# Attention per head pair with weight sums inverted through DMA, and an MLP woven in by hand

## The chip, the cores and the metric

The kernel runs on one core of one Trainium2 chip. The metric is the device time of one execution in microseconds (us), from the first to the last instruction on that core. The engines of the core are named as the profile names them: PE (TensorE, matmuls; PEld is its weight loading), DVE (VectorE), ACT (ScalarE), POOL (GpSimd) and SP (SyncE, which here only issues transfers). Each engine takes its instructions in one fixed order; an instruction that waits holds up everything behind it on that engine.

## The reference

Softmax attention for 8 batches of 12 heads (448 tokens, 64 values a head), and a two-layer MLP with a leaky ReLU over the 3584 tokens that come out, 768 to 2048 to 768. All inputs and the output are fp32.

```python
def _attn_ref(q, k, v):                      # (8, 12, 448, 64) each
    scale = 1.0 / np.sqrt(q.shape[-1])
    scores = scale * np.matmul(q, k.transpose(0, 1, 3, 2))
    scores = scores - np.max(scores, axis=-1, keepdims=True)
    attn = np.exp(scores)
    attn = attn / (np.sum(attn, axis=-1, keepdims=True) + 1e-09)
    return np.matmul(attn, v).astype(np.float32)

def _moe_ref(x, w_in, w_out):                # x (3584, 768), w_in (768, 2048), w_out (2048, 768)
    h = x @ w_in
    g = np.maximum(0.01 * h, h)
    return (g @ w_out).astype(np.float32)
```

The inputs are small (q, k and v are normal draws times 0.1), and neither kernel subtracts the row maximum.

## The kernel before

Both weight matrices are loaded first, one transfer each, from POOL's queue, which casts fp32 to bf16 on the way. Then a loop over the 8 batches: `attn_batch(b)` traces the attention of batch b, and `mlp_batch(b - 1)` the MLP of the batch before. The order on each engine is made by the framework's scheduler from the dependencies; so matmuls of the MLP fill gaps of the attention, but no line of the kernel says where.

Attention goes by head pairs (`hp`, 6 a batch). For each head, q, k and v come by one casting transfer each (L77, L81, L85), 112 tokens on the partitions in four chunks (`so`); the tile of v also gets 64 columns of ones (L75). q and k of the two heads lie side by side, so a transpose by PE (L94, L97) of a 112 x 128 chunk puts head 0 on partitions 0 to 63 and head 1 on 64 to 127; DVE copies each chunk out (L95, L98). Then for each head: four score matmuls, keys down and queries across, over 64 rows of the array (L106); each is followed by Exp on ACT (L112); four matmuls of values with Exp's output (L117) gather in `pvpsum`, where rows 64 to 127 hold the sum of the weights 64 times over, from the ones. The sum is inverted on ACT as exp(-ln(sum)) (L126, L128), and DVE multiplies (L129) into `xT`, the transposed attention output.

The MLP of a batch (448 tokens) has 16 groups of six matmuls (L140) with Prelu on ACT (L146), and then eight groups of 16 matmuls (L151), each giving 112 tokens by 384 outputs, copied by DVE (L158) and stored from SP's queue (L159).

All PSUM pools have two buffers: `ps_tr` (transposes), `ps_sc` (scores), `ps_pv` (values) and `ps_mm` (MLP).

Of the kernel before, what the change touches and what calls it, by code (L numbers as in the profile page):

```python
# [1 line left out]

# [6 lines left out]

F32 = mybir.dt.float32  # L10
BF16 = mybir.dt.bfloat16
AX = mybir.ActivationFunctionType


@with_exitstack
def kernel(
    ctx: ExitStack,
    tc: tile.TileContext,
    q: bass.AP,
    k: bass.AP,  # L20
    v: bass.AP,
    moe_w_in: bass.AP,
    moe_w_out: bass.AP,
    out: bass.AP,
):
    nc = tc.nc

    B, H, S, D = q.shape
    DM, DF = moe_w_in.shape
    NTOK = B * S  # L30
    assert H * D == DM

    P = 128
    HP = H // 2
    SC = 112
    NSC = S // SC
    KD = DM // P
    MD = DF // P
    scale = 1.0 / float(D) ** 0.5

    const_pool = ctx.enter_context(tc.tile_pool(name="const", bufs=1))
    w_pool = ctx.enter_context(tc.tile_pool(name="weights", bufs=1))

    ident = const_pool.tile([P, P], BF16)
    make_identity(nc, ident)

    w_in_sb = w_pool.tile([P, KD, DF], BF16)
    nc.gpsimd.dma_start(
        out=w_in_sb, in_=moe_w_in.rearrange("(ko ki) n -> ki ko n", ki=P)
    )  # L50
    w_out_sb = w_pool.tile([P, MD, DM], BF16)
    nc.gpsimd.dma_start(
        out=w_out_sb, in_=moe_w_out.rearrange("(ko ki) n -> ki ko n", ki=P)
    )

    ld_pool = ctx.enter_context(tc.tile_pool(name="ld", bufs=2))
    qkT_pool = ctx.enter_context(tc.tile_pool(name="qkT", bufs=2))
    exp_pool = ctx.enter_context(tc.tile_pool(name="exp", bufs=2))
    pv_pool = ctx.enter_context(tc.tile_pool(name="pv", bufs=3))
    xT_pool = ctx.enter_context(tc.tile_pool(name="xT", bufs=2))  # L60
    h_pool = ctx.enter_context(tc.tile_pool(name="h", bufs=2))
    o_pool = ctx.enter_context(tc.tile_pool(name="o", bufs=4))

    ps_tr = ctx.enter_context(tc.tile_pool(name="ps_tr", bufs=2, space=bass.MemoryType.PSUM))
    ps_sc = ctx.enter_context(tc.tile_pool(name="ps_sc", bufs=2, space=bass.MemoryType.PSUM))
    ps_pv = ctx.enter_context(tc.tile_pool(name="ps_pv", bufs=2, space=bass.MemoryType.PSUM))
    ps_mm = ctx.enter_context(tc.tile_pool(name="ps_mm", bufs=2, space=bass.MemoryType.PSUM))

    def attn_batch(b, xT):
        for hp in range(HP):  # L70
            h0 = 2 * hp
            q_sb = ld_pool.tile([SC, NSC, 2, D], BF16, tag="q")
            k_sb = ld_pool.tile([SC, NSC, 2, D], BF16, tag="k")
            v_sb = ld_pool.tile([SC, NSC, 2, 2 * D], BF16, tag="v")
            nc.vector.memset(v_sb[:, :, :, D:], 1.0)  # L75
            for jh in range(2):
                nc.gpsimd.dma_start(  # L77
                    out=q_sb[:, :, jh, :],
                    in_=q[b, h0 + jh].rearrange("(so si) d -> si so d", si=SC),
                )  # L80
                nc.gpsimd.dma_start(  # L81
                    out=k_sb[:, :, jh, :],
                    in_=k[b, h0 + jh].rearrange("(so si) d -> si so d", si=SC),
                )
                nc.gpsimd.dma_start(  # L85
                    out=v_sb[:, :, jh, :D],
                    in_=v[b, h0 + jh].rearrange("(so si) d -> si so d", si=SC),
                )

            qT_sb = qkT_pool.tile([P, S], BF16, tag="qT")  # L90
            kT_sb = qkT_pool.tile([P, S], BF16, tag="kT")
            for so in range(NSC):
                qps = ps_tr.tile([P, SC], BF16, tag="tr")
                nc.tensor.transpose(qps, q_sb[:, so], ident[:SC, :SC])  # L94
                nc.vector.tensor_copy(qT_sb[:, ts(so, SC)], qps)  # L95
                kps = ps_tr.tile([P, SC], BF16, tag="tr")
                nc.tensor.transpose(kps, k_sb[:, so], ident[:SC, :SC])  # L97
                nc.vector.tensor_copy(kT_sb[:, ts(so, SC)], kps)  # L98

            for jh in range(2):  # L100
                h = h0 + jh
                pl = jh * D
                expT = exp_pool.tile([SC, NSC, S], BF16)
                for so in range(NSC):
                    spsum = ps_sc.tile([SC, S], F32, tag="sc")
                    nc.tensor.matmul(  # L106
                        spsum,
                        kT_sb[pl:pl + D, ts(so, SC)],
                        qT_sb[pl:pl + D, :],
                        start=True, stop=True,  # L110
                    )
                    nc.scalar.activation(  # L112
                        expT[:, so, :], spsum, AX.Exp, scale=scale
                    )
                pvpsum = ps_pv.tile([2 * D, S], F32, tag="pv")
                for so in range(NSC):
                    nc.tensor.matmul(  # L117
                        pvpsum,
                        v_sb[:, so, jh, :],
                        expT[:, so, :],  # L120
                        start=(so == 0), stop=(so == NSC - 1),
                    )
                kc = h // 2
                po = (h % 2) * D
                lns = pv_pool.tile([D, S], F32, tag="lns")
                nc.scalar.activation(lns, pvpsum[D:, :], AX.Ln)  # L126
                rec = pv_pool.tile([D, S], F32, tag="rec")
                nc.scalar.activation(rec, lns, AX.Exp, scale=-1.0)  # L128
                nc.vector.tensor_mul(  # L129
                    xT[po:po + D, kc, :], pvpsum[:D, :], rec  # L130
                )

    def mlp_batch(b, xT):
        NN = 2
        NW = DM // NN
        h_sb = h_pool.tile([P, MD, S], BF16)
        for m in range(MD):
            mpsum = ps_mm.tile([P, S], F32, tag="mm")
            for kk in range(KD):
                nc.tensor.matmul(  # L140
                    mpsum,
                    w_in_sb[:, kk, ts(m, P)],
                    xT[:, kk, :],
                    start=(kk == 0), stop=(kk == KD - 1),
                )
            nc.scalar.activation(h_sb[:, m, :], mpsum, AX.Prelu, alpha=0.01)  # L146
        for sq in range(NSC):
            for n in range(NN):
                opsum = ps_mm.tile([SC, NW], F32, tag="mm")
                for m in range(MD):  # L150
                    nc.tensor.matmul(  # L151
                        opsum,
                        h_sb[:, m, ts(sq, SC)],
                        w_out_sb[:, m, ts(n, NW)],
                        start=(m == 0), stop=(m == MD - 1),
                    )
                osb = o_pool.tile([SC, NW], F32, tag="osb")
                nc.vector.tensor_copy(osb, opsum)  # L158
                nc.sync.dma_start(  # L159
                    out=out[ds(b * S + sq * SC, SC), ts(n, NW)], in_=osb  # L160
                )

    xTs = [None] * B
    for b in range(B):
        xTs[b] = xT_pool.tile([P, KD, S], BF16, name="xT")
        attn_batch(b, xTs[b])
        if b > 0:
            mlp_batch(b - 1, xTs[b - 1])
    mlp_batch(B - 1, xTs[B - 1])


# [28 lines left out]
```

## Time and profile before

| what | number |
|---|---|
| three runs | 921.73, 922.72, 918.97 us; median 921.73 |
| profiled execution, its span | 923.2 us; no other time of its own is given |
| PE busy | 807.8 us (88%), 2944 matmuls |
| ACT busy | 592.9 us (64%), 193 of its 897 instructions are table loads |
| DVE, POOL busy | 181.9 us (20%), 203.3 us (22%) |
| mean granted TensorE clock | 0.752 |
| read from HBM, written | 45.61 MB, 11.01 MB |

The page of the profile is of one execution. Its shares of busy time are averages over stages with different limits. Further views used below: the chain of work that ended last, the groups of instructions by line, a table of busy time by stretch with the clock that PE was granted, and the instructions in order of time, where a bracket at the end of a row gives the idle time of the engine before it and who ended it.

### The profile page before, as it was taken

To read this page: it belongs to the slowest core of one execution; us is meant where nothing else is said; L and a number is where in the kernel's file an instruction comes from. 1 tells how busy PE (TensorE), PEld (TensorE's weight loads), DVE (VectorE), ACT (ScalarE), POOL (GpSimd) and SP (SyncE) were. 2 spreads that over 40 slices of the span, in tenths; PEclk is the share of its full clock that TensorE was granted. 3 is DMA by queue.
4 is the path that set the end of the run, shared out by engine and by line. 5 is a ranking of instruction groups with operands and counts; after the bars stand their busy time and mean duration, and the time that the engine had idled before them with its cause. 6 is when DMAs were issued, how large, how long until landed. Compare 5 with 4: busy or idle time off the path is not lost.

```text
span 923.2 us, 8367 instructions
## 1 busy us (share of the span) xinstructions
PE 807.8 (88%) x2944; PEld 336.8 (36%) x2944; DVE 181.9 (20%) x592; ACT 592.9 (64%) x897; POOL 203.3 (22%) x296
## 2 busy tenths in 40 slices
PE   0477789989899999999899998999989999999998
PEld 0122222236222552226322372224622255222656
DVE  0122212112212122211221122211222112120101
ACT  0188888871888538882688808886288844888130
POOL 3323232211332023210323103320132202310000
PEclk9999999979555895559755596557955588555999
DMA  9944343313443144322434115431343314410102
GB/s 179 141 25 29 25 31 20 26 12 65 29 30 21 27 59 31 20 16 43 47 26 30 11 53 42 26 20 18 63 30 26 20 28 58 30 11 0 43 18 60
DMA packets 144713, 34.36 MB, mean 37 GB/s; under 512 B 134688, under 2 KB 143904, under 8 KB 144672
## 3 DMA queue, kind: packets, MB, share of 16 engines
q0 software_dynamic: 136480, 22.83, 31.9%
q1 hardware_dynamic: 8192, 11.01, 4.0%
q8 instruction: 23, 0.38, 0.2%
q14 instruction: 18, 0.15, 0.1%
HBM read 45.61 MB, written 11.01 MB: 61 GB/s over the span
## 4 chain that ended last, share of the span: by engine, by line
PE 55%; ACT 33%; issue 6%; DMA 3%; POOL 1%; DVE 0%; POOLq 0%; ACTq 0%
PE opsum L151 18%; PE spsum L106 13%; PE mpsum L140 12%; ACT L112 12%; PE pvpsum L117 10%; ACT expT L112 9%; ACT lns L126 5%; ACT L126 4%; DMA q_sb<-in_q_dram 3%; PE qps L94 1%; ACT L128 1%; ACT h_sb L146 1%; PE kps L97 1%; ACT rec L128 0%; DVE v_sb L75 0%
## 5 line engine op out<-in xcount | busy, mean ns | idle before, releaser
L112 ACT ACTIVATE expT<-spsum 112x448 bf16<-112x448 f32 x384 | 195.1, 535 | 219.2 <-PE spsum L106 218.1
L140 PE MATMUL mpsum<-xT,w_in_sb 128*128 128x448 bf16 x768 | 287.3, 486 | 8.8 <-ACT h_sb L146 8.7
L106 PE MATMUL spsum<-qT_sb,kT_sb 64*112 64x448 bf16 x384 | 216.9, 569 | 66.0 <-ACT expT L112 65.8
L117 PE MATMUL pvpsum<-expT,v_sb 112*128 112x448 bf16 x384 | 206.2, 545 | 0.1
L151 PE MATMUL opsum<-w_out_sb,h_sb 128*112 128x384 bf16 x1024 | 167.7, 326 | 0.0
L151 PEld LDWEIGHTS <-h_sb 128*112 128x112 bf16 x1024 | 133.3, 130 | 33.8
L85 POOL DMA_DIRECT2D v_sb<-in_v_dram x96 | 67.0, 701 | 328.8 <-PE pvpsum L117 268.0
L106 PEld LDWEIGHTS <-kT_sb 64*112 64x112 bf16 x384 | 60.5, 160 | 207.0 <-issue 205.8
L126 ACT ACT_TABLE_LOAD x96 | 123.2, 1283 | 1.7
L77 POOL DMA_DIRECT2D q_sb<-in_q_dram x96 | 67.2, 702 | 251.3 <-PE kps L97 211.4
L146 ACT ACTIVATE h_sb<-mpsum 128x448 bf16<-128x448 f32 x128 | 68.1, 537 | 80.8 <-PE mpsum L140 80.5
L112 ACT ACT_TABLE_LOAD x90 | 115.5, 1283 | 2.3 <-PEq L184 0.7
L140 PEld LDWEIGHTS <-w_in_sb 128*128 128x128 bf16 x768 | 86.1, 122 | 76.4 <-issue 55.3
L117 PEld LDWEIGHTS <-v_sb 112*128 112x128 bf16 x384 | 43.5, 115 | 169.5 <-issue 164.9
L129 DVE TENSOR_TENSOR xT<-pvpsum,rec 64x448 bf16<-64x448 f32 x96 | 59.0, 615 | 222.2 <-ACT rec L128 222.2
L94 PE MATMUL qps<-ident,q_sb 112*128 112x112 bf16 x192 | 53.9, 281 | 35.7 <-DMA q_sb<-in_q_dram 35.7
L95 DVE COPY qT_sb<-qps 128x112 bf16<-128x112 bf16 x192 | 40.4, 210 | 221.6 <-PE spsum L106 130.5
L81 POOL DMA_DIRECT2D k_sb<-in_k_dram x96 | 67.2, 702 | 43.0 <-PE kps L97 26.5
L158 DVE COPY osb<-opsum 112x384 f32<-112x384 f32 x64 | 35.6, 557 | 166.7 <-PE opsum L151 154.5
L128 ACT ACTIVATE rec<-lns 64x448 f32<-64x448 f32 x96 | 54.1, 563 | 0.1
L97 PE MATMUL kps<-ident,k_sb 112*128 112x112 bf16 x192 | 53.1, 276 | 0.8
L126 ACT ACTIVATE lns<-pvpsum 64x448 f32<-64x448 f32 x96 | 51.8, 540 | 2.0 <-PE pvpsum L117 0.8
(13 smaller groups left out, 122.3 us busy)
## 6 DMA issues: line engine op xcount, KB each, us to landing
out_dram<-osb SPq DMA_DIRECT2D x64, 168.0 KB, 2.1
q_sb<-in_q_dram POOLq DMA_DIRECT2D x96, 56.0 KB, 2.7
k_sb<-in_k_dram POOLq DMA_DIRECT2D x96, 56.0 KB, 2.9
v_sb<-in_v_dram POOLq DMA_DIRECT2D x96, 56.0 KB, 2.7
w_in_sb<-in_moe_w_in_dram POOLq DMA_DIRECT2D x1, 3072.0 KB, 17.8
w_out_sb<-in_moe_w_out_dram POOLq DMA_DIRECT2D x1, 3072.0 KB, 31.5
```

The lines of the kernel that those rows point to most:

```text
L77: nc.gpsimd.dma_start(out=q_sb[:, :, jh, :], in_=q[b, h0 + jh].rearrange("(so si) d -> si so d", si=SC),)
L81: nc.gpsimd.dma_start(out=k_sb[:, :, jh, :], in_=k[b, h0 + jh].rearrange("(so si) d -> si so d", si=SC),)
L85: nc.gpsimd.dma_start(out=v_sb[:, :, jh, :D], in_=v[b, h0 + jh].rearrange("(so si) d -> si so d", si=SC),)
L94: nc.tensor.transpose(qps, q_sb[:, so], ident[:SC, :SC])
L106: nc.tensor.matmul(spsum, kT_sb[pl:pl + D, ts(so, SC)], qT_sb[pl:pl + D, :], start=True, stop=True,)
L112: nc.scalar.activation(expT[:, so, :], spsum, AX.Exp, scale=scale)
L117: nc.tensor.matmul(pvpsum, v_sb[:, so, jh, :], expT[:, so, :], start=(so == 0), stop=(so == NSC - 1),)
L126: nc.scalar.activation(lns, pvpsum[D:, :], AX.Ln)
L128: nc.scalar.activation(rec, lns, AX.Exp, scale=-1.0)
L140: nc.tensor.matmul(mpsum, w_in_sb[:, kk, ts(m, P)], xT[:, kk, :], start=(kk == 0), stop=(kk == KD - 1),)
L146: nc.scalar.activation(h_sb[:, m, :], mpsum, AX.Prelu, alpha=0.01)
L151: nc.tensor.matmul(opsum, h_sb[:, m, ts(sq, SC)], w_out_sb[:, m, ts(n, NW)], start=(m == 0), stop=(m == MD - 1),)
```

## The change

The whole body is rewritten with an order that is given by the text of the kernel (`tc.manual_schedule()`). The arithmetic is the same, with these differences.

- **Loads.** `load(u)` brings q, k and v of a head pair (u = 0 to 47) as fp32, one transfer for both heads, in rows of four tokens; `cast(u)` converts on GpSimd with four copies (q, k, and v for each head). Tokens so lie in another order, which the store undoes. The first pairs are loaded ahead of the weights, which come in eight pieces, two with each of the first four pairs. Four v tiles with ones are kept and written once; head 1 has its ones in columns 0 to 63.
- **Transposes.** All eight of a pair go to one PSUM tile, with one DVE copy of 896 columns.
- **Scores.** For each chunk of keys, a matmul for head 0 (rows 0 to 63 of the array) and one for head 1 (rows 64 to 127) follow each other, into two banks; one Exp takes both.
- **Sums.** DVE copies the value product to SBUF. One row of it, the sums, goes by a transfer to 112 partitions (`bc_t`), DVE inverts it (`recips`), a transfer writes the inverses to DRAM and two transfers read them back as 64 equal rows each (`rb`). DVE then multiplies (`muls`). All of these transfers are issued from SP, as the stores are. Ln and the second Exp are gone.
- **MLP.** Blocks of 384 or 512 tokens (`cuts`), so that each output group has 128 tokens; a block can take tokens of two batches.
- **Order.** A pair has eight slots; after each slot a share of the matmuls of the block before is emitted, in proportion to the work left. The first eight pairs have no MLP beside them, and the last block has no attention.

```diff
+    cuts = [((b * S) // P) * P for b in range(B)] + [B * S]
+    ctx.enter_context(tc.manual_schedule())
...
+    ps_s = ctx.enter_context(tc.tile_pool(name="ps_s", bufs=2, space=PSUM))
+    ps_tr = ctx.enter_context(tc.tile_pool(name="ps_tr", bufs=1, space=PSUM))
+    ps_pv = ctx.enter_context(tc.tile_pool(name="ps_pv", bufs=1, space=PSUM))
+    ps_mm = ctx.enter_context(tc.tile_pool(name="ps_mm", bufs=2, space=PSUM))
...
+    def load(u):
...
+        for a, name in ((q, "fq"), (k, "fk"), (v, "fv")):
+            t = ld_pool.tile([SC, 2, NSC, D], F32, name=name)
+            nc.gpsimd.dma_start(
+                out=t.rearrange("p h so d -> p h (so d)"),
+                in_=a[b, 2 * hp:2 * hp + 2].rearrange("h (p so) d -> p h (so d)", so=NSC),
+            )
...
+    def cast(u):
...
+        nc.gpsimd.tensor_copy(q_sb[u].rearrange("p so h d -> p h so d"), fq)
+        nc.gpsimd.tensor_copy(k_sb[u].rearrange("p so h d -> p h so d"), fk)
+        for j in range(2):
+            nc.gpsimd.tensor_copy(v_sb[u % NV][:, j, :, j * D:(j + 1) * D], fv[:, j])
+
+    load(0)
+    cast(0)
+    load(1)
+    load(2)
+    load(3)
+    cast(1)
+    for i in range(4, 6):
+        load(i)
...
+    def transposes(u):
...
+                nc.tensor.transpose(
+                    tr[:, i, ts(so, SC)], src[:, so], ident[:SC, :SC]
                 )
+        qk_t[u] = qk_pool.tile([P, 2, S], BF16, name="qkT")
+        nc.vector.tensor_copy(qk_t[u], tr)
...
+    def scores(u, c):
+        ps = ps_s.tile([SC, 2, 512], F32, name="sc")
...
+        for j in range(2):
+            nc.tensor.matmul(
+                ps[:, j, :S],
+                qk_t[u][j * D:(j + 1) * D, 1, ts(c, SC)],
+                qk_t[u][j * D:(j + 1) * D, 0, :],
+                start=True, stop=True,
+            )
...
+        nc.scalar.activation(e_t[u][:, :, c, :], sc_t.pop((u, c))[:, :, :S], AX.Exp, scale=scale)
+
+    def pv(u, j):
...
+        t = t_pool.tile([P, S], F32, name=f"t{j}")
+        nc.vector.tensor_copy(t, ps)
...
+        row = t[D:D + 1, :] if j == 0 else t[0:1, :]
+        nc.sync.dma_start(out=bc_t[u][:, j, :], in_=row)
+
+    def recips(u):
+        rec = r_pool.tile([SC, 2, NSC], F32, name="rec")
+        nc.vector.reciprocal(rec, bc_t[u])
+        d = d_pool.tile([2, S], F32, name="d")
+        nc.sync.dma_start(out=d.rearrange("j (p c) -> p j c", c=NSC), in_=rec)
+        rb = r_pool.tile([P, S], F32, name="rb")
+        for j in range(2):
+            nc.sync.dma_start(out=rb[ts(j, D), :], in_=d[j:j + 1, :].to_broadcast([D, S]))
+        bc_t[u] = rb
+
+    def muls(u):
...
+            for i in (b, b + 1):
...
+                nc.vector.tensor_mul(
+                    x[pl, hp, a - cuts[i]:z - cuts[i]],
+                    pv_s[u, j][pl, a - lo:z - lo],
+                    bc_t[u][pl, a - lo:z - lo],
                 )
...
-                lns = pv_pool.tile([D, S], F32, tag="lns")
-                nc.scalar.activation(lns, pvpsum[D:, :], AX.Ln)
-                rec = pv_pool.tile([D, S], F32, tag="rec")
-                nc.scalar.activation(rec, lns, AX.Exp, scale=-1.0)
...
+    def mlp(i):
+        n = cuts[i + 1] - cuts[i]
...
+            for kk in range(KD):
                 nc.tensor.matmul(
+                    ps[:, :n], w_in_sb[:, kk, ts(m, P)], get_xT(i)[:, kk, :n],
                     start=(kk == 0), stop=(kk == KD - 1),
                 )
+                if kk == KD - 1:
+                    nc.scalar.activation(h[:, m, :n], ps[:, :n], AX.Prelu, alpha=0.01)
+                yield n
+        for c in range(n // P):
...
+                        ps[:, :NW], h[:, m, ts(c, P)], w_out_sb[:, m, ts(w, NW)],
...
+                        nc.vector.tensor_copy(o[:, ts(w, NW)], ps[:, :NW])
+                    yield NW
+            store(o, cuts[i] + c * P)
...
+        def s0():
+            if on:
+                scores(u, 0)
+                scores(u, 1)
+                expo(u, 0)
+            load(u + 6)
+            if u < 6:
+                load_w(2)
+
+        def s1():
+            if on:
+                expo(u, 1)
+            if u >= 2:
+                recips(u - 2)
+
+        def s2():
+            if 1 <= u <= NU:
+                pv(u - 1, 0)
+
+        def s3():
+            cast(u + 2)
+
+        def s4():
+            if on:
+                scores(u, 2)
+                scores(u, 3)
+                expo(u, 2)
+
+        def s5():
+            if on:
+                expo(u, 3)
+
+        def s6():
+            if 1 <= u <= NU:
+                pv(u - 1, 1)
+
+        def s7():
+            if u + 1 < NU:
+                transposes(u + 1)
+            if u >= 2:
+                muls(u - 2)
...
+    transposes(0)
+    for i in range(B + 1):
+
+        first = 0 if i == 0 else HP * i + 2
+        last = HP * (i + 1) + 2 if i < B else first
+        work = [s for u in range(first, min(last, NU + 2)) for s in slots(u)]
+        atoms = mlp(i - 1) if i > 0 else iter(())
...
+        for n, s in enumerate(work):
+            s()
+            while used < total * (n + 1) // len(work):
...
```

213 lines of the change are left out of this document (110 added, 103 removed).

## The prediction

> **What bounds the kernel now.** First the page: the shares, and the chain of work that ended last, by engine.
>
> ```profile
> span 923.2 us, 8367 instructions
> ...
> PE 807.8 (88%) x2944; PEld 336.8 (36%) x2944; DVE 181.9 (20%) x592; ACT 592.9 (64%) x897; POOL 203.3 (22%) x296
> ...
> PE 55%; ACT 33%; issue 6%; DMA 3%; POOL 1%; DVE 0%; POOLq 0%; ACTq 0%
> ```
>
> PE is busy nearly always, yet a third of the chain is ACT. What a busy PE does shows in the table by stretch: three stretches of one batch period, the MLP's second half, the start of the next attention, its rest (columns: length; busy time of PE, PEld, DVE, ACT, POOL; granted clock; DMA share; GB/s).
>
> ```profile
> 203.00:224.00 21.00, 21.00 (x131) 16.76 (x129) 3.91 (x7) 0.54 (x1) 0.00 (x0) 1.00 0.19 58
> 224.00:232.00 8.00, 8.00 (x47) 3.40 (x44) 3.44 (x17) 4.79 (x9) 2.85 (x5) 1.00 0.53 51
> 232.00:308.00 76.00, 69.47 (x185) 20.60 (x185) 15.41 (x54) 64.32 (x97) 20.83 (x30) 0.51 0.36 23
> ```
>
> 47 matmuls in 8 us at clock 1.00, then 185 in 76 us at 0.51: 2.4 a microsecond against 5.9, with PE 91% busy and ACT 85%. The 88% is slow work. The order of time, and two short stretches, show what lies at the turns:
>
> ```profile
> 231.53 0.54 PE L140 MATMUL mpsum<-xT,w_in_sb 128*128 128x448 bf16 x2
> 232.41 1.28 ACT L112 ACT_TABLE_LOAD   x1
> 234.30 0.53 PE L106 MATMUL spsum<-qT_sb,kT_sb 64*112 64x448 bf16 x1 [2.23 <-ACT expT L112]
> 232.00:236.00 4.00, 1.77 (x7) 0.74 (x7) 0.97 (x4) 3.62 (x7) 2.72 (x4) 0.65 0.78 50
> 196.56 1.33 PE L140 MATMUL mpsum<-xT,w_in_sb 128*128 128x448 bf16 x3
> 198.80 2.00 PE L140 MATMUL mpsum<-xT,w_in_sb 128*128 128x448 bf16 x9
> 199.00:199.50 0.50, 0.50 (x5) 0.20 (x2) 0.32 (x1) 0.48 (x2) 0.20 (x1) 0.94 0.00 0
> ```
>
> A change of table (Ln to Exp) takes 1.28 us; scores wait for the Exp behind it, PE idles 2.23 us, and inside those 4 us the clock falls, to 0.65 on their mean and 0.50 after. It comes back (0.94 at 199.0) after matmuls that ran without a gap since 196.56. So the bound is a chain of Ln, table, Exp and scores, which besides holds the clock down.
>
> **The change, priced.** Durations at full clock, from the tail and from the one full-speed attention stretch:
>
> ```profile
> 880.35 18.16 PE mpsum L140 x96
> 898.51 20.81 PE opsum L151 x128
> 226.56 0.58 PE L106 MATMUL spsum<-qT_sb,kT_sb 64*112 64x448 bf16 x2
> 227.08 0.22 PE L94 MATMUL qps<-ident,q_sb 112*128 112x112 bf16 x1
> 227.14 0.21 PE L97 MATMUL kps<-ident,k_sb 112*128 112x112 bf16 x1
> 227.98 0.36 PE L117 MATMUL pvpsum<-expT,v_sb 112*128 112x448 bf16 x1
> 228.28 0.39 PE L106 MATMUL spsum<-qT_sb,kT_sb 64*112 64x448 bf16 x1
> 228.60 0.36 PE L117 MATMUL pvpsum<-expT,v_sb 112*128 112x448 bf16 x1
> 228.80 0.21 PE L94 MATMUL qps<-ident,q_sb 112*128 112x112 bf16 x1
> ```
>
> A 448-column matmul takes 18.16/96 = 0.189 us, a 384-column one 20.81/128 = 0.163, a 512-column one by the same slope 0.216. Value products start to transposes 228.60 to 228.80: 0.20, nothing extra. Into 64-row scores 227.98 to 228.28 is 0.30, 0.11 extra; out again 0.32, 0.13 extra. A transpose follows the other after 0.06.
>
> **MLP.** Blocks are now 384 and 512 tokens by turns, in 128-token output rows. 384: 96 x 0.163 + 96 x 0.163 = 31.2 us; 512: 96 x 0.216 + 128 x 0.163 = 41.6. Seven are woven: 4 x 31.2 + 3 x 41.6 = 249.6. The last 512 stands alone.
>
> **Attention on PE, per head pair.** Value products 8 x 0.189 = 1.51. Scores in two groups of four, 64-row matmuls on two row halves by turns: each group costs 0.24 for going in and out, and four matmuls between 2 x 0.19 (halves side by side) and 4 x 0.19. So 1.24 to 2.0; no row shows two halves at once, and I take the middle, 1.6. Eight transposes 0.06 apart, or up to twice that, as nothing long hides their weight loads: 0.5 to 1.0, taken 0.6. Together 3.7; 40 pairs (8 to 47) stand in the woven part: 148.
>
> The Trainium skill, "TensorEngine Tiling (Array Packing)", Key Properties, says that changing the tiling mode drains TensorE, which speaks against the four switches of row shape that a pair makes around its scores; the 0.11 and 0.13 above are what this trace shows of it. "TensorE: Matmul & The Clock Gate", Part 3, says that tiles on different rows run at the same time; by it the pair costs 1.24 and the whole 14 us less, by the serial row 16 us more.
>
> **Off the path.** Groups that price the other engines:
>
> ```profile
> L112 ACT ACTIVATE expT<-spsum 112x448 bf16<-112x448 f32 x384 | 195.1, 535 | 219.2 <-PE spsum L106 218.1
> L126 ACT ACT_TABLE_LOAD x96 | 123.2, 1283 | 1.7
> L112 ACT ACT_TABLE_LOAD x90 | 115.5, 1283 | 2.3 <-PEq L184 0.7
> L146 ACT ACTIVATE h_sb<-mpsum 128x448 bf16<-128x448 f32 x128 | 68.1, 537 | 80.8 <-PE mpsum L140 80.5
> L129 DVE TENSOR_TENSOR xT<-pvpsum,rec 64x448 bf16<-64x448 f32 x96 | 59.0, 615 | 222.2 <-ACT rec L128 222.2
> L95 DVE COPY qT_sb<-qps 128x112 bf16<-128x112 bf16 x192 | 40.4, 210 | 221.6 <-PE spsum L106 130.5
> L158 DVE COPY osb<-opsum 112x384 f32<-112x384 f32 x64 | 35.6, 557 | 166.7 <-PE opsum L151 154.5
> L77 POOL DMA_DIRECT2D q_sb<-in_q_dram x96 | 67.2, 702 | 251.3 <-PE kps L97 211.4
> ...
> 0.32 0.10 POOL L184 MEMSET const-bfloat16-1.0<- 128x1 bf16 x1
> 0.74 0.20 POOL masks.py:197 MEMSET ident<- 128x128 bf16 x1 [0.29 <-POOLq L184]
> 2.36 0.30 POOL masks.py:199 TENSOR_SCALAR_AFFINE_SELECT ident<-ident 128x128 bf16<-128x128 bf16 x1
> ```
>
> ACT: the table loads (239 us in these two rows) go but for one, as with Ln gone only Exp and Prelu are left, and no load stands at Prelu's line; per pair four Exp of 2 x 0.535 at most and 2.7 Prelu of 0.54 leave 5.7 us. DVE: two value copies of 0.6, the 896-column transpose copy (0.6 to 1.3, between the rates of the 112- and 384-column rows), three multiplications of 0.6 on average, a short reciprocal, 1.2 output copies: about 4.8. GpSimd: three loads of 0.70, and casts of 1536 columns in four copies; the three small rows give 0.1 plus 0.8 to 1.6 ns a column, so 1.6 to 2.9, taken 2.3: 4.4. PE's pair is 249.6/42 + 3.7 = 9.6. All three are covered by PE, twice over.
>
> **Waits left on PE.** Scores follow their transposes by one slot of MLP, 249.6/(7 x 48) = 0.74 us, which covers the 896-column copy or leaves up to 0.6; an Exp ahead of a Prelu can hold one of the two MLP banks. I take 0.5 a pair (0 to 1.5): 20. Each block's first matmuls want the last pair's multiplications: 1 us x 7 (0 to 3).
>
> Woven: 249.6 + 148 + 20 + 7 = 425.
>
> **Start and end.**
>
> ```profile
> q_sb<-in_q_dram POOLq DMA_DIRECT2D x96, 56.0 KB, 2.7
> out_dram<-osb SPq DMA_DIRECT2D x64, 168.0 KB, 2.1
> w_out_sb<-in_moe_w_out_dram POOLq DMA_DIRECT2D x1, 3072.0 KB, 31.5
> 5.86 29.74 DMA q_sb<-in_q_dram
> ```
>
> The 29.74 us wait behind the weights goes. GpSimd has made the identity at 2.7 us (above), so pair 0 is ready at about 2.7 + 2.1 + 2.7 + 2.3 = 9.8; three more pairs' loads (6.3), a cast, two pairs' loads (4.2) and then 2.1 + 1.4 (two weight pieces, as two more transfers) + 2.3 a pair bring pair 2 at 28. Pairs 2 to 7 have no MLP beside them, and a new loop holds DVE: reciprocal, write (2.1), broadcast (2.1 to 2.9), multiplications (1.8), next reciprocal, since all stand in one order on DVE. That is 7 us a pair: 28 + 42 = 70. Bounds 55 (loop half hidden) and 85 (landings slowed by the weights, which take some 31 us of transfers then). The end: 41.6 for the last block, and as now 923.2 - (898.5 + 20.8) = 3.9 behind the last matmul: 45.5.
>
> **Sum:** 70 + 425 + 45.5 = 540 us, against the span of 923.2, which stands 0.2% above the median of 921.73. Ends, with pairs of 3.2 and 4.5 on PE: 55 + 249.6 + 128 + 45.5 = 478, and 85 + 249.6 + 180 + 60 + 21 + 45.5 = 641.
>
> **Rivals.**
>
> *The clock stays low, in part or all.* Against it: PE has no wait near 2.2 us left, and at half clock it would be its own bound, gapless between scores, as the 2.4 us before 199.0 were. For it: 76 us at 91% busy (232 to 308) never brought the clock back. All low: 2 x (249.6 + 148) + 7 + 70 + 45.5 = 918, no change; low now and then 640 to 880. Since the trace halves the clock at a wait of 2.23, a late broadcast or cast would be enough, and the rival keeps a tenth. The Trainium skill, "TensorE: Matmul & The Clock Gate", HAM oscillation, puts the limit at an idle window of about 3.4 us; by it waits of 2 to 3 us would cost no clock, and this trace differs.
>
> *Slower: the inversion loop binds everywhere.* DVE stands at the multiplications until the broadcast has landed, and behind it wait the value copies and output copies that free PE's banks. At 7 us it hides under a pair of 9.6. It decides over 48 pairs only from (923 - 45 - 9)/48 = 18 us, landings near 8 us each; the rows have 2.1 to 2.9 outside the weight loading. Then 930 and more.
>
> *Scores are not side by side.* 2.0 a pair: 556, inside the range.
>
> **Chances.** Forecast 540 with its bounds 0.82; clock low at times 0.07 (640 to 880); low throughout 0.03 (918); inversion loop slower 0.03; below 478 0.05 (a start near 45 us and scores side by side). The bounds, rounded outward, hold 8 in 10: 470 to 645. A run tells from no change about 0.5%. Faster 0.95 (of the low clock throughout a third), same 0.02, slower 0.03.
>
> **What would show it.** One table load; clock near 1.00 from about 80 us on; PE without waits over 1 us in the woven part; 384-column matmuls 0.163 apart; score pairs starting together or 0.19 apart; DVE's longest wait at the multiplications in the first 70 us only; a block of 41.6 at the end. Wrong if the granted clock is 0.5 between 100 and 450 us, if GpSimd's casts take over 5 us a pair, or if PE waits for DVE every pair.

## The result, and the profile after

The changed kernel takes 555.78 us (median of four runs, 551.72 to 557.13) against 921.36 for the kernel before on the same chip: ratio 0.602, 95% interval 0.599 to 0.605. The profiled execution took 556.75 us, with a span of 555.0. The prediction was 540, with a range of 470 to 645. Every median here is of the executions within 1.5% of their kernel's fastest, which leaves out one of the version in the scheduler's order (607.42 us) and three of four of the version with a quarter of the weights (544.53 to 548.50).

The page of the changed kernel: span, busy times of the engines, the granted clock in 40 slices, the chain that ended last, and four groups.

```profile
span 555.0 us, 7636 instructions
...
PE 478.5 (86%) x2816; PEld 237.6 (43%) x2816; DVE 215.2 (39%) x400; ACT 231.3 (42%) x321; POOL 202.1 (36%) x350
...
PEclk9998555999989999999799999999899999997999
...
PE 65%; DMA 22%; DVE 7%; SPq 2%; issue 2%; POOL 2%; DVEq 0%; POOLq 0%
...
L233 PE MATMUL mm<-xT,w_in_sb 128*128 128x384 bf16 (+1 forms) x768 | 173.0, 364 | 20.9 <-DVE xT L208 19.4
...
L109 POOL CAST v<-fv 112x256 bf16<-112x256 f32 x96 | 38.3, 404 | 230.9 <-PE pv L176 230.6
...
L106 POOL CAST q<-fq 112x512 bf16<-112x512 f32 x48 | 34.0, 708 | 4.2 <-PE tr L148 1.5
...
L107 POOL CAST k<-fk 112x512 bf16<-112x512 f32 x48 | 31.8, 662 | 0.1
```

ACT is gone from the chain, where it had a third, and its busy time fell from 592.9 to 231.3. In its place stands DMA with 22%, about 120 us, where the sum had only the 42 us of the loop in the start. The clock is recorded at half from about 55 to 97 us (the fifth to seventh slice), and dips a little further on; the matmuls themselves run at about half pace earlier, as four value products take 1.68 us at 32.53 and 0.92 at 103.20. GpSimd's casts take 2 x 0.404 + 0.708 + 0.662 = 2.2 us a pair.

Where the DMA share lies, the order of time shows (start, length, work, in brackets the idle time before it and who ended it):

```profile
39.06 1.41 DVE L208 TENSOR_TENSOR xT<-t,rb 64x384 bf16<-64x384 f32 x4 [7.51 <-DMA rb<-d]
...
55.25 0.69 DVE L208 TENSOR_TENSOR xT<-t,rb 64x384 bf16<-64x384 f32 x2 [10.73 <-DMA rb<-d]
...
59.35 1.65 PE L176 MATMUL pv<-e,v 112*128 112x448 bf16 x4 [11.25 <-DVE t L181]
...
95.63 1.78 PE L233 MATMUL mm<-xT,w_in_sb 128*128 128x384 bf16 x5
```

The table by stretch (columns as before):

```profile
40.00:60.00 20.00, 6.57 (x26) 2.58 (x26) 5.75 (x12) 3.45 (x4) 10.04 (x17) 0.79 1.17 232
```

The list of transfers (KB each, median us from issue to landing):

```profile
w_in_sb<-in_moe_w_in_dram POOLq DMA_DIRECT2D x4, 768.0 KB, 12.7
```

In the start DVE stands at the multiplications until the broadcast has landed, 7.5 and 10.7 us, and PE stands behind DVE's copy of the values for 11.25. Such a wait holds two landings in a row: the write is issued at 27.57 and the broadcast, which waits for it, at 33.55, 6.0 us later; the multiplication begins another 5.5 behind that. For the fifth pair, when the weights are in, the two take 1.5 and 2.9 (83.61, 85.08, 88.01). From 40 to 60 us the transfer engines are busy throughout (share 1.17, 232 GB/s), with weight pieces that take 12.7 us to land. The MLP begins at 95.63 us.

The woven part, one stretch of its order of time:

```profile
122.20 0.62 DVE L152 COPY qkT<-tr 128x896 bf16<-128x896 bf16 x1 [0.42 <-PE tr L148]
...
122.88 0.59 PE L160 MATMUL sc<-qkT 64*112 64x448 bf16 x4
123.40 1.48 PE L245 MATMUL mm<-w_out_sb,h 128*128 128x384 bf16 x8
...
130.70 0.62 DVE L152 COPY qkT<-tr 128x896 bf16<-128x896 bf16 x1 [0.42 <-PE tr L148]
```

A pair takes 130.70 - 122.20 = 8.5 us with no idle time on PE; a group of four score matmuls holds it 123.40 - 122.88 = 0.52. Where a 512-token block begins, it looks otherwise; here the three woven ones, and the last:

```profile
152.43 0.38 PE L233 MATMUL mm<-xT,w_in_sb 128*128 128x512 bf16 x1 [2.29 <-DVE xT L208]
...
273.71 1.60 PE L233 MATMUL mm<-xT,w_in_sb 128*128 128x512 bf16 x3 [5.83 <-DVE xT L208]
...
393.20 1.60 PE L233 MATMUL mm<-xT,w_in_sb 128*128 128x512 bf16 x3 [4.55 <-DVE xT L208]
...
500.57 1.24 PE L233 MATMUL mm<-xT,w_in_sb 128*128 128x512 bf16 x5
506.38 22.90 PE L233 MATMUL mm<-xT,w_in_sb 128*128 128x512 bf16 x91 [4.57 <-DVE xT L208]
529.12 20.96 PE L245 MATMUL mm<-w_out_sb,h 128*128 128x384 bf16 x128
```

The table by stretch behind the second of these waits:

```profile
274.00:278.00 4.00, 4.00 (x13) 1.51 (x12) 1.08 (x3) 0.73 (x2) 0.40 (x1) 0.62 0.38 99
278.00:282.00 4.00, 4.00 (x22) 1.66 (x20) 0.16 (x1) 3.17 (x5) 0.13 (x1) 1.00 0.25 58
```

The block's first matmuls wait for the last pair's multiplications, which wait for their broadcast; behind the wait 13 matmuls fill 4 us, where 22 do at full clock. The broadcast of this turn goes out among the loads of a pair:

```profile
264.94 0.66 POOL L94 DMA_DIRECT2D fq<-in_q_dram  x1
...
265.85 1.12 SPq L195 DMA_DIRECT2D rb<-d  x2
```

Its two halves reach DVE 4.8 and 7.2 us behind the issue (multiplications at 270.65 and 273.04). In the last block no pair is loaded any more, and there it is 3.0 (502.04 to 505.06).

### The profile page after: what moved, and what is told of

Read it like the earlier page. It is cut to its first block, busy times and chain, and to the rows that moved or that the text cites. A ratio compares the mean times of both kernels' runs of the same rounds, so it can differ in the third digit from the quotient of the medians.

```text
span 555.0 us, 7636 instructions
## 1 busy us (share of the span) xinstructions
PE 478.5 (86%) x2816; PEld 237.6 (43%) x2816; DVE 215.2 (39%) x400; ACT 231.3 (42%) x321; POOL 202.1 (36%) x350
## 4 chain that ended last, share of the span: by engine, by line
PE 65%; DMA 22%; DVE 7%; SPq 2%; issue 2%; POOL 2%; DVEq 0%; POOLq 0%
PE mm L233 25%; PE mm L245 19%; PE pv L176 11%; DMA d<-rec 8%; DMA sums<-t 7%; DMA rb<-d 7%; PE sc L160 6%; DVE xT L208 3%; PE tr L148 3%; DVE qkT L152 2%; SPq L195 1%; DVE o L250 1%; DMA fv<-in_v_dram 1%; SPq L224 1%; POOL fq L94 0%
## 5 line engine op out<-in xcount | busy, mean ns | idle before, releaser
L170 ACT ACTIVATE e<-sc 112x896 bf16<-112x896 f32 x192 | 168.5, 915 | 188.8 <-PE sc L160 188.6
L233 PE MATMUL mm<-xT,w_in_sb 128*128 128x384 bf16 (+1 forms) x768 | 173.0, 364 | 20.9 <-DVE xT L208 19.4
L245 PE MATMUL mm<-w_out_sb,h 128*128 128x384 bf16 x896 | 162.1, 326 | 0.8 <-DVE o L250 0.6
L176 PE MATMUL pv<-e,v 112*128 112x448 bf16 x384 | 100.9, 390 | 29.9 <-DVE t L181 29.9
L181 DVE COPY t<-pv 128x448 f32<-128x448 f32 x96 | 59.6, 620 | 149.0 <-PE pv L176 148.7
L238 ACT ACTIVATE h<-mm 128x384 bf16<-128x384 f32 (+1 forms) x128 | 69.9, 546 | 109.2 <-PE mm L233 109.1
L208 DVE TENSOR_TENSOR xT<-t,rb 64x384 bf16<-64x384 f32 (+2 forms) x144 | 87.1, 630 | 68.2 <-DMA rb<-d 67.0
L245 PEld LDWEIGHTS <-h 128*128 128x128 bf16 x896 | 83.6, 98 | 67.0 <-issue 13.7
L176 PEld LDWEIGHTS <-v 112*128 112x128 bf16 x384 | 38.9, 103 | 74.7 <-issue 47.8
L160 PE MATMUL sc<-qkT 64*112 64x448 bf16 x384 | 63.4, 411 | 8.6 <-DVE qkT L152 6.4
## 6 DMA issues: line engine op xcount, KB each, us to landing
w_in_sb<-in_moe_w_in_dram POOLq DMA_DIRECT2D x4, 768.0 KB, 12.7
```

Of the source, the lines that this page charges most:

```text
L160: nc.tensor.matmul(ps[:, j, :S], qk_t[u][j * D:(j + 1) * D, 1, ts(c, SC)], qk_t[u][j * D:(j + 1) * D, 0, :], start=True, stop=True,)
L170: nc.scalar.activation(e_t[u][:, :, c, :], sc_t.pop((u, c))[:, :, :S], AX.Exp, scale=scale)
L176: nc.tensor.matmul(ps, v_sb[u % NV][:, j, c, :], e_t[u][:, j, c, :], start=(c == 0), stop=(c == NSC - 1),)
L181: nc.vector.tensor_copy(t, ps)
L208: nc.vector.tensor_mul(x[pl, hp, a - cuts[i]:z - cuts[i]], pv_s[u, j][pl, a - lo:z - lo], bc_t[u][pl, a - lo:z - lo],)
L233: nc.tensor.matmul(ps[:, :n], w_in_sb[:, kk, ts(m, P)], get_xT(i)[:, kk, :n], start=(kk == 0), stop=(kk == KD - 1),)
```

## Experiments

The first five take the change apart: what of the 366 us is the inversion, what the order and the rest of the structure. The next five ask why the sum came out as it did: the start, the scores, the casts, the turns. The last two put together what gained.

### The kernel before, with a reciprocal on DVE

```diff
-                nc.scalar.activation(lns, pvpsum[D:, :], AX.Ln)
-                nc.scalar.activation(rec, lns, AX.Exp, scale=-1.0)
+                nc.vector.reciprocal(rec, pvpsum[D:, :])
```

> The kernel before with one part of the change alone: the weight sums are inverted by a DVE reciprocal read from PSUM, in place of Ln and Exp on ACT; all 193 table loads but one go. Theory A (the chain of table loads and waits, and the half clock that it causes, is what bounds before): PE keeps the full clock, a batch period falls from 109 to some 75 to 85 us, and the time to 640 to 720 us, most of the way to the changed kernel. Rival B (the order by hand and the denser matmuls matter most, the scheduler's order leaves PE with waits anyway): over 800 us, clock in attention still near 0.5. If a reciprocal of 448 columns takes DVE some 4 us, DVE gets 2 x 4 + 2.4 us a pair, and waits on DVE take the place of those on ACT.

Measured: 693.22 us, ratio 0.751 (0.749 to 0.753), clock 0.99 in the profiled execution. Busy times and the new group:

```profile
PE 602.4 (88%) x2944; PEld 308.0 (45%) x2944; DVE 457.9 (67%) x688; ACT 272.7 (40%) x513; POOL 203.2 (30%) x296
...
L126 DVE RECIPROCAL rec<-pvpsum 64x448 f32<-64x448 f32 x96 | 277.9, 2929 | 51.6 <-PE pvpsum L117 51.6
```

With Ln and the table loads gone, and nothing else of the change made, 229 of the 366 us are won and the clock is back. The reciprocal is dear: 2.93 us for 448 columns, where a multiplication takes 0.62.

### The kernel before, with no inversion at all

```diff
-                lns = ...; rec = ...            # Ln, Exp
-                nc.vector.tensor_mul(xT[po:po + D, kc, :], pvpsum[:D, :], rec)
+                nc.vector.tensor_copy(xT[po:po + D, kc, :], pvpsum[:D, :])
```

> The kernel before with the division left out: the numerators are copied to xT undivided, so no Ln, no Exp, no reciprocal and no trip (that part of the computation is missing). Theory 1 (what the old structure, its order by the scheduler and its single heads, costs is beside the inversion): 620 to 690 us; the 693 of the version with a DVE reciprocal would then have at most some 70 us of reciprocal in it, and at least 65 us of the gain come from rows side by side, paired loads and the order. Rival (the 278 us of reciprocals were what held that version at 693): without them the old structure comes to 555 to 590, near the changed kernel. Granted clock 0.95 or more by both.

It leaves out the division: the numerators go on undivided.

Measured: 637.01 us, ratio 0.692 (0.690 to 0.694).

```profile
PE 594.7 (94%) x2944; PEld 301.9 (48%) x2944; DVE 180.6 (28%) x592; ACT 260.8 (41%) x513; POOL 202.8 (32%) x296
...
PEclk9999999999999999999999999999999999999999
```

The first theory holds. In the old structure the inversion with all that hangs on it costs 921.3 - 637.0 = 284 us; what is left is bound by PE at full clock. The new structure is at 555.8 with its inversion in it, so at least 81 us of the gain are not the inversion; no run divides them up, and the 35.8 us that PE waits for the first load behind the weights are still in the 637. The reciprocals cost 56 of the 693.

### The changed kernel, with Ln and Exp on ACT

```diff
-        rec, d, rb ...                          # sums, reciprocal, write, broadcast by DMA
+        for j in range(2):
+            nc.scalar.activation(lns[ts(j, D), :], pv_s[u, j][ts(1 - j, D), :], AX.Ln)
+        nc.scalar.activation(rb, lns, AX.Exp, scale=-1.0)
```

> The changed kernel with Ln and Exp on ACT put back in place of the trip through DMA (both heads of a pair together: two Ln, one Exp of 128 rows, two table loads a pair). ACT gets 2 x 1.28 + 3 x 0.55 = 4.2 us a pair more, near 10 us against PE's 8.5 to 10.5. Theory A: scores wait 2 to 3 us behind the tables, the clock falls in places, 600 to 700 us; the first eight pairs get faster (no loop through DMA), by some 25 us. Rival B (order by hand suffices, ACT has room): within 3% of the changed kernel or faster by the 25 us of the start.

Measured: 590.15 us, ratio 0.640 (0.638 to 0.642). The page's busy times and one of two equal groups (L187 has 48 loads more):

```profile
PE 492.6 (84%) x2816; PEld 240.8 (41%) x2816; DVE 222.4 (38%) x352; ACT 430.7 (73%) x561; POOL 196.9 (34%) x350
...
L189 ACT ACT_TABLE_LOAD x48 | 61.6, 1283 | 0.9
```

The waits (us in all, times, longest), and the first MLP matmuls in the order of time:

```profile
PE mm L227 <- ACT h L232: 55.7, 21, 3.6
```

```profile
73.24 2.74 PE L227 MATMUL mm<-xT,w_in_sb 128*128 128x384 bf16 x8
```

Only 34 us more than through DMA, between the two forecasts. Two table loads a pair are covered in part, since the rest of ACT leaves room; the wait that came with them is PE's 55.7 us at Prelu, not the one of the scores that was forecast. But the MLP begins at 73.24 instead of 95.63: in the start the trip through DMA *loses* 22 us, and so wins 34 + 22 = 57 behind it.

### The changed kernel, with reciprocals on DVE

```diff
-        rec, d, rb ...
+        for j in range(2):
+            nc.vector.reciprocal(rb[ts(j, D), :], pv_s[u, j][ts(1 - j, D), :])
```

> The changed kernel with the trip through DMA replaced by two DVE reciprocals of 64 x 448 from SBUF, written to the other half's partitions. Theory A on the start (the first 96 us are a loop of transfers that land late behind the weights): the loop is gone and the start falls to some 60 us, bound by GpSimd and DVE, the wait of 4 to 6 us at block turns goes too. If a reciprocal takes 0.6 us: 500 to 515 us. If it takes about 4 us: DVE has 13 us a pair, over PE's 9, and the kernel takes 640 to 700 us: then the trip through DMA earns its place. Rival B: the start is bound by GpSimd's loads and casts, no gain: 550 to 560 us.

Measured: 641.55 us, ratio 0.695 (0.692 to 0.699). The chain, and the group:

```profile
DVE 68%; PE 26%; POOL 3%; issue 2%; DMA 1%; POOLq 0%
...
L187 DVE RECIPROCAL rb<-t 64x448 f32<-64x448 f32 x96 | 282.7, 2945 | 2.4
```

DVE becomes the bound: 5.9 us of reciprocals a pair on top of its other work. It binds the start too: with no trip through DMA in it, the first MLP matmul stands at 96.18 us, where some 60 was expected. What the trip buys is the shape: the sums of a head are one row of 448, which a transfer lays out as 112 partitions by 4, and there the reciprocal of both heads takes 0.2 us.

### The changed kernel in the scheduler's order

```diff
-    ctx.enter_context(tc.manual_schedule())
```

> The changed kernel without its order by hand: the same instructions, ordered by the framework's scheduler from the same text. Theory A (the order by hand keeps PE fed, but the removal of the table loads is the larger part): 580 to 680 us, with more and longer PE waits and the clock low in places. Rival B (order matters little once ACT's chain is gone): 540 to 570 us.

Measured: 597.43 us, ratio 0.647 (0.644 to 0.650). A row of the waits in the changed kernel, and two in this one:

```profile
DVE xT L208 <- DMA rb<-d: 67.0, 27, 10.7
```

```profile
DVE xT L207 <- DMA rb<-d: 140.0, 53, 11.2
...
PEld L159 <- DVE qkT L151: 68.9, 47, 5.2
```

The order by hand is worth 42 us. Left to the dependencies, DVE waits 140 us for broadcasts instead of 67 and the scores wait for their transposes.

### A quarter of the weights

```diff
-    w_in_sb = w_pool.tile([P, KD, DF], BF16)
+    w_in_sb = w_pool.tile([P, KD, DF // 4], BF16)    # w_out_sb likewise; each quarter is used four times
```

It leaves out three quarters of both weight matrices' transfers.

> The changed kernel, with only a quarter of each weight matrix loaded and used for all four quarters of the products: matmuls as before, six of the eight weight transfers left out (9.4 of 12.6 MB). Theory A: the inversion's transfers land in 2 to 3 us in the start as later, the pairs 2 to 7 take 7 us each in place of 8 to 18, the first MLP matmul comes at 65 to 75 us in place of 95.6, the whole 525 to 535 us. Rival B: the loop is as long without the weights (fixed cost of each transfer), start over 88 us, over 548 us in all.

Measured: 533.96 us in one execution. The profile is of another, of 548.50 us, so no ratio is given and only its start is read; where the 14.5 us between the two lie is not on record.

```profile
58.31 2.52 DVE L208 TENSOR_TENSOR xT<-t,rb 64x384 bf16<-64x384 f32 x4 [1.15 <-DMA rb<-d]
...
66.23 2.38 DVE L208 TENSOR_TENSOR xT<-t,rb 64x384 bf16<-64x384 f32 x4 [1.30 <-DMA rb<-d]
...
74.36 2.73 DVE L208 TENSOR_TENSOR xT<-t,rb 64x384 bf16<-64x384 f32 x4 [0.94 <-DMA rb<-d]
...
81.91 1.78 PE L233 MATMUL mm<-xT,w_in_sb 128*128 128x384 bf16 x5
```

The MLP begins at 81.9 instead of 95.6, between the theory (65 to 75) and its rival (over 88). So in this execution the missing weights shorten the start by 14 us; as only the longer execution has a profile, the 14 is no firm size. With the weight pieces landed a pair still takes 66.23 - 58.31 = 7.9 and 8.1 us in the loop. Part of this is PE's half pace, as four value products take 1.65 us here (61.87), not 0.92.

### Scores by head, and scores on one half

Two kernels on the score matmuls. One issues them head by head, so that neighbours lie on the same rows; the other puts both heads on head 0's rows (head 1's weights are then those of head 0).

```diff
-        for j in range(2):                     # head 0, head 1, head 0, head 1
+        for j in range(2):                     # head 0 twice, then head 1 twice
+            for c in (c0, c0 + 1):
```

> The changed kernel with one part undone: the four score matmuls of a slot go head by head (two on rows 0 to 63, then two on rows 64 to 127), so that only the middle two stand on different rows. Theory A (matmuls on different rows run side by side: in the trace after, a group of four holds PE 0.52 us in place of 0.89): a group gets 0.19 us longer, a pair 0.38, 40 woven pairs 15 us: 568 to 574 us. Rival B (they run one after the other in either order, the gain is elsewhere): within 3 us of the changed kernel.

```diff
-                qk_t[u][j * D:(j + 1) * D, 1, ts(c, SC)],
-                qk_t[u][j * D:(j + 1) * D, 0, :],
+                qk_t[u][0:D, 1, ts(c, SC)],
+                qk_t[u][0:D, 0, :],
```

> The changed kernel with both heads' score matmuls on head 0's 64 rows, so that none can lie beside another (head 1's weights are then those of head 0). Theory 1 (a group of four holds PE 0.52 us because two matmuls on different row halves run together): a group takes 0.85 to 0.95 us, and about 80 woven groups of 96 with 0.37 us more each, 30 us, give 580 to 592 us. Rival (64-row matmuls simply start closer together than 0.19 us, or the records mislead): groups stay at 0.52 and the time within 5 us of 556.

Measured: by head 560.43 us, ratio 0.607 (0.605 to 0.609); on one half 569.62, ratio 0.618 (0.616 to 0.619). A group of scores and the matmul behind it, first by head, then on one half:

```profile
119.30 0.59 PE L161 MATMUL sc<-qkT 64*112 64x448 bf16 x4
119.82 1.48 PE L234 MATMUL mm<-xT,w_in_sb 128*128 128x384 bf16 x8
```

```profile
116.91 0.96 PE L160 MATMUL sc<-qkT 64*112 64x448 bf16 x4
117.80 1.47 PE L233 MATMUL mm<-xT,w_in_sb 128*128 128x384 bf16 x8
```

On one half the group holds PE 0.89 us, by head 0.52 as in the changed kernel. So matmuls on different halves do run side by side, and the order within the group doesn't matter, against the expectation, by which a group by head would take 0.19 longer. The 4.7 us of the version by head above the changed kernel are under a per cent, with intervals that touch, and their cause is open. "TensorE: Matmul & The Clock Gate" of the Trainium skill, Part 3, says that tiles on different rows run together, with which the 0.52 against 0.89 agrees, and that matmuls start and end strictly in order; with that the 0.52 by head does not sit well, as two matmuls of one half stand first there, and the four yet start in twos, 6 and 7 ns apart. What lets the other half go ahead was not tried.

On one half, some 80 woven groups add 0.37 each, 30 us of PE's work, but the time rises by 13.8. The waits give back the difference: of the four long waits at block turns in the changed kernel only the last is left:

```profile
519.00 22.68 PE L233 MATMUL mm<-xT,w_in_sb 128*128 128x512 bf16 x91 [4.25 <-DVE xT L208]
```

A pair that is 0.7 us longer does not cover a wait of 5.8 by itself. The landings are shorter too: at these three turns the broadcast goes out 0.8 to 1.4 us ahead of a pair's loads (273.41 against 274.81 at the second), and the first multiplication begins 2.8 to 3.0 us behind it. In the changed kernel the loads begin 0.5 us behind the broadcast at the first turn, 0.9 and 0.7 ahead of it at the second and third, with waits of 2.3, 5.8 and 4.6 us. This order of things is read from the traces; no run moved the loads alone.

### Casts by the loading transfers

```diff
-        nc.gpsimd.tensor_copy(q_sb[u].rearrange("p so h d -> p h so d"), fq)     # and k, v
+        nc.gpsimd.dma_start(out=t[:, :, j, :],                                   # bf16, per head: q, k, v
+                            in_=a[b, 2 * hp + j].rearrange("(p so) d -> p so d", so=NSC))
```

> The changed kernel with one part undone: q, k and v are cast by the loading transfers again, one transfer for each head, and the GpSimd copies are gone (eight v tiles and eight bf16 tiles of q and k take the place of the fp32 ones). Theory A (loads and casts lie off the path but in the start): GpSimd saves 2.2 us of casts and adds 2.0 us of issuing a pair; the woven part stays at 405 us; the start moves by less than 10 us, bound by the inversion's trips: 545 to 565 us. Rival B (casting transfers of 256-byte rows crowd the DMA engines and delay the inversion): 580 us or more, with the landing of the broadcast over 4 us in the woven part too.

Measured: 542.85 us, ratio 0.588 (0.584 to 0.592), 13 us less than the changed kernel and 2 below the range of the theory. The multiplications of 448 columns, groups kept apart by shape, in the changed kernel and then in this one:

```profile
L208 DVE TENSOR_TENSOR xT<-t,rb 64x448 bf16<-64x448 f32 x48 | 35.3, 735 | 33.3 <-DMA rb<-d 32.8
```

```profile
L205 DVE TENSOR_TENSOR xT<-t,rb 64x448 bf16<-64x448 f32 x48 | 29.6, 618 | 26.6 <-DMA rb<-d 25.8
```

Its first MLP matmuls:

```profile
89.53 1.78 PE L230 MATMUL mm<-xT,w_in_sb 128*128 128x384 bf16 x5
```

Without copies on GpSimd the same multiplication takes 0.618 us instead of 0.735, and the start is 6 us shorter. "GPSIMD Engine Reference" of the Trainium skill, Specifications, says that GpSimd and VectorE contend for SBUF where VectorE has two SBUF inputs; the trace agrees, with 0.12 us a multiplication. The changed kernel's own trace says the same: its 74 multiplications, of any width, that meet no copy of GpSimd take at most 0.62 us, as all 144 do here, and the 70 that overlap one up to 1.95.

How the 13 us hang on this is less sure. About 6 are in the start and 6 in PE's waits at the three woven turns, 12.7 us in the changed kernel and 6.7 here; but the loads changed along with the copies, in number, kind and buffers, so the shares of the two are not separated.

### Multiplications and blocks a pair later

```diff
-            if u >= 2: muls(u - 2)
+            if u >= 3: muls(u - 3)              # blocks begin at pair 6 i + 3; one weight piece a pair
```

> The changed kernel with the multiplications of a pair one pair later (three pairs behind its scores, not two), the MLP blocks one pair later with them, and the weights' eight pieces spread over eight pairs, one each, not two in each of four. Theory A (in the start and at the block turns DVE stands at the multiplications until the broadcast lands, and PE behind it): the start's pairs fall from 11 us to the 6 of GpSimd's loads and casts, nine of them end near 65 to 72 us; the waits of 2 to 6 us at the seven turns and the half clock after them go (some 25 us): 500 to 520 us. Rival B (the loop only moves, DVE waits one pair later): within 10 us of the changed kernel.

Measured: 535.77 us, ratio 0.581 (0.579 to 0.583), 20 us less than the changed kernel; theory (500 to 520) and rival both missed. From the page the clock, from the waits DVE's longest, and the first MLP matmuls:

```profile
PEclk9865556899999999999999999999999999999999
```

```profile
DVE rec L190 <- DMA sums<-t: 85.3, 27, 12.4
```

```profile
101.79 1.70 PE L233 MATMUL mm<-xT,w_in_sb 128*128 128x384 bf16 x8
```

The waits at the turns are gone, and with them every dip of the clock behind the start. The start itself is 6 us longer, where it was expected to fall to 65 to 72: nine pairs stand in it, and DVE now waits for the sums to land. The reason shows on SP, whose transfers keep one order: the write is issued at 27.61, the broadcast that waits for it at 33.93, the next pair's sums behind that at 35.10, and DVE's reciprocal begins at 42.08. On the start the rival was right: the loop only moved.

### Both together, and the start on ACT

The last two are versions meant to be fast: casts by transfers and the later multiplications in one; and this with Ln and Exp on ACT for the first six pairs.

> The changed kernel with the casts done by the loading DMAs, and the multiplications and the MLP blocks a pair later, weight pieces one a pair: the two versions that were faster, in one. Theory (their gains come from different places: DVE's and GpSimd's shared time and the start in one, waits at the block turns and the clock in the other): 520 to 530 us, clock 0.98 or more, first MLP matmul at 92 to 100 us. Rival (both removed the same waits at the turns): 534 to 543.

```diff
+        if u < NA:                              # NA = 6: no transfer of the sums
+            ... Ln of both heads, one Exp (as above); multiplications two pairs later
```

> As the version that joins the two, but the sums of the first six pairs are inverted by Ln and Exp on ScalarE, with the multiplications two pairs later; from pair 6 on through DMA, three pairs later. Theory (the start is bound by landings of 7 to 12 us under the weight transfers, and ScalarE is idle there): first MLP matmul at 68 to 78 us, 495 to 512 us in all, 6 + 6 or up to 12 pairs of table loads. Rival (the weights bound the start by themselves, about 31 us of transfers at full rate for each matrix seen in the kernel before, some 65 to 95 us after their first issue): first MLP or its w_out half still waits, no more than 5 us gained on the joined version.

Measured, in this order: 526.05 us, ratio 0.571 (0.568 to 0.573), and 508.62, ratio 0.552 (0.550 to 0.554). Of the joined version the first MLP matmul, of the last one the same, and the stretches before and behind it:

```profile
96.97 1.47 PE L230 MATMUL mm<-xT,w_in_sb 128*128 128x384 bf16 x8
```

```profile
66.24 2.42 PE L241 MATMUL mm<-xT,w_in_sb 128*128 128x384 bf16 x7
```

```profile
30.00:66.00 36.00, 25.55 (x116) 10.68 (x114) 15.97 (x35) 35.59 (x44) 28.65 (x42) 0.64 1.57 170
80.00:100.00 20.00, 14.24 (x85) 7.22 (x83) 6.24 (x12) 8.00 (x14) 14.57 (x22) 0.83 1.34 116
```

The gains of the two nearly add: 12.9 and 20.0 apart, 29.7 together, as forecast; the clock is not (0.938, where 0.98 was said), as the start stays at half. The first MLP matmul then comes 30.7 us earlier with ACT in the start, which ACT now fills (35.59 of 36 us). Of that 17.4 stay: one pair fewer stands before that matmul, and in the later stretch, where the pairs change over to the trip, PE is idle for 5.8 of 20 us, while DVE waits 9.7 for sums to land. So the start is bound by ACT now, not by the weights. This version takes 47 us off the changed kernel, 413 off the one before.

## Why the prediction came out as it did

The sum was 70 + 425 + 45.5 = 540; the trace has 95.6 + 404.9 + 54.4 = 555.0 (MLP from 95.63, last block from 500.57). The main step holds: tables, Exp and scores off the path, clock back (full from about 100 us on but for the turns, where 80 was said), PE the bound. Three terms were off, with errors that partly cancel; that the sum came within 3% is in part luck.

- **Start, 70 and at most 85; measured 95.6.** The mis-sized term, outside its own bounds. Pair 2 came at 25.0, where 28 was said; the loop of six pairs, put at 42 us, took 70.6. The loop was there as described (DVE stands at the multiplications), but priced at 7 us a pair with landings from rows outside the weight loading, and with PE at full clock; under it write and broadcast landed in 5.5 to 8.1 us each for the first three pairs, not in 2.1 to 2.9, and DVE's waits were 7.5 to 10.7 us. The upper bound was meant for landings slowed by the weights and was set too low. In the one profile without three quarters of the weights 14 of the 26 us are gone, and a pair of the loop takes 7.9 to 8.1, not 7; the rest is not divided. The two versions with Ln and Exp in the start, whose MLP begins at 73.2 and 66.2, show that the landings held it and the weights alone did not.
- **Woven part, 425; measured 404.9.** MLP as priced. A pair costs 8.5 us at 384 tokens, less 31.2/6 = 5.2 of MLP: 3.3, where 3.7 and waits of 0.5 were put. Of this the scores are about 1.2 (two groups of 0.52, and 0.09 on going into each), the low end that stood for halves side by side and was taken as 1.6, and the waits are nil: the transposes' copy of 896 columns took 0.62 us, the low end, and fits under its slot of MLP. By 249.6 + 40 x 3.3 = 382, 23 us are left for the turns and the end of the low clock, which were put at 7. So the errors of this term cancel in part: 16 less for attention, 20 less for waits in the pairs, 16 more at the turns.
- **Turns.** The step "1 us x 7" failed: 2.3 to 5.8 us each where a 512-token block begins. Reciprocal, write and broadcast of the last pair stand between the second and the eighth slot of the same pair: 6/8 of 8.5 = 6.4 us in a 384-token block, 7.6 in a 512-token one, where a pair takes 41.6/6 + 3.3 = 10.2. So it is the block behind the short pairs that waits. How long depends on the landing: with 6.9 us (pairs of 9.2, scores on one half) three of the four turns have no wait over 0.8, but there the broadcasts also land sooner, ahead of a pair's loads. The last turn stands behind a pair with no attention left, 6/8 of 5.2 = 3.9. Behind the wait the clock is low for some 4 us. The version with multiplications a pair later takes both away.
- **End, 45.5; measured 54.4.** A turn again: 4.57 us of wait, 91 matmuls in 22.90 us instead of 91 x 0.216 = 19.7, and 4.9 instead of 3.9 behind the last matmul.
- **Off the path.** GpSimd's casts are 2.2 us a pair (put at 2.3). That they were covered was right for GpSimd; that they cost nothing elsewhere was not, as they slow DVE's multiplications. The version without them, with other loads, is 13 us faster.
- **Rivals.** The low clock did not come, though dips behind the turn waits are its small form. The loop did not bind everywhere: 8.5 us of PE's pair cover it at the landings outside the start. "Scores not side by side" was put 16 us above the forecast; the kernel with scores on one half came out 13.8 above the changed one, by another sum (30 more of work, 16 given back at the turns).

The sum priced the new kernel from the ground up and never said which part of the change brings what; the experiments say it in two parts: 284 us hung on the inversion and the clock, and 81 or more on the rest: loads, order, pairing and rows side by side.

## What to carry to other kernels

Price a round trip through DMA at the stage where it runs: landings of 2 to 3 us became 5 to 8 under bulk loads, two of them stand in a row, and an engine that waits in order hands this to every other. What saves in the steady part can cost in the start; one kernel may use both ways, by stage. A one-row result is cheap to process only once it is spread over partitions, and a consumer should stand as many steps behind a transfer as its slowest landing needs, at the turns above all.

## What the runs showed of the hardware that was not expected

- A reciprocal on DVE costs 2.93 us for 448 columns, 4.7 times a multiplication, from PSUM or SBUF alike; 8 columns take 0.20.
- Copies on GpSimd slow DVE's multiplications with two SBUF inputs from 0.618 to 0.735 us.
- Score matmuls on two row halves overlap whichever way the four are ordered.
- A wait of 5.83 us on PE is followed by 4 us at clock 0.62 on the mean, a wait of 2.29 (before 152.43) by 0.57 from 154 to 158; in both the next 4 us are at 1.00.
- The record of the clock can miss a stretch: with scores on one half it stays at 1.00 up to 97 us, yet four value products take 1.65 us at 61.12, as in the changed kernel at clock 0.50.
